# Eight weight transfers on a paced queue, and a new written-out order, in a kernel of sparse attention and a rational MLP

## The chip, the cores and the metric

The kernel runs on one core of a Trainium2 chip. The metric is the device time of one execution in microseconds. An execution profiled by the hardware gives the span from its first to its last instruction and the rows below.

## The reference

Inputs are q, k, v of shape (8 batches, 8 heads, 576 rows, 64), weights W_in (512 x 2048) and W_out (2048 x 512), and a few coefficients, all float32.

- Attention with two masks: heads 0 to 3 see the last 32 positions (the local half, L), heads 4 to 7 the positions with the same remainder modulo 32 (the strided half, S). Scores are scaled by 1/8, softmax as usual, then the product with v.
- The heads are laid side by side: x has 4608 rows of 512.
- h = x W_in; P = a0 + a1 h + a2 h^2 + a3 h^3; Q = 1 + |b0||h| + |b1| h^2; the output is (P / Q) W_out, 4608 x 512, float32.

## The kernel before

`graph` writes the work down as numbered operations with their dependences; nothing is decided at run time. Five lists (`ORDER`) give each engine its operations in order: PE (products and transposes), ACT, DVE, POOL (transfers that cast float32 to bf16) and SP (plain and transposing transfers). `SIDE` gives each movable copy, zero fill, eviction and |h| to ACT (a) or DVE (d), `AT` gives each tile in PSUM its bank. `emit` puts a semaphore wait ahead of an operation where its engine does not yet know that a dependence is done. Every engine and every queue is in order: an operation that waits holds all that stand behind it.

Batch 0 is cast straight into SBUF in two parts of 8 and 10 blocks of 32 rows and turned by PE, so is batch 1 (`stage0`, `stage1`, L379 to L446). From batch 2 on POOL casts q and k to DRAM (`casts`, L448) and v to SBUF (`casts_v`, L460), and SP loads q and k transposed (`loads`, L481) and shifts v (L473). Batch 2's casts wait for the last reader of W_in's fourth quarter in chunk 1, later ones for the loads of the batch before.

The MLP (`mlp`, L1123) works in chunks of 256, 256, then 512 rows. W_in products (L1166) fill PSUM, an eviction (helper L314) makes h; then |h| (L1184 on ACT, L1188 on DVE), Q in two DVE steps, Ln and Exp on ACT for 1/Q, P in five DVE steps, and the last product g (L1219). W_out products (L1236) follow in four operations for each 128 rows, each over 512 of the 2048 middle columns, then eviction and store (L1256).

The weights go through `weights` (L477) on POOL: W_in in four transfers of 512 columns, W_out in two of 1024 rows. A W_in operation waits for the quarter that it reads, a W_out operation for the half. None of the six transfers waits for anything but POOL's order. In that order the quarters of W_in are 21st, 25th, 30th and 31st (second, first, fourth, third), W_out's halves 34th and 37th, directly ahead of batch 2's casts.

The other early transfers, as they write bf16, by size: a cast of batch 0's q or k 128 KB (first part) or 160 (second), of batch 1's 288; a piece of V 32 or 40 for batch 0 and 72 for later ones; a quarter of W_in 512, a half of W_out 1024.

`F` and the last loop hold fill products, which compute nothing that is read; 39 of the 47 stand ahead of the first W_in product.

Of the kernel before, what the change touches and what calls it, by code (L numbers as in the profile page):

```python
# [208 lines left out]
def graph(nc, q, k, v, w_in, w_out, pa, pb, out):  # L209
# [15 lines left out]
    P = Prog(nc)  # L225
# [18 lines left out]
    Win = sb("Win", [128, NK1, Fmid])  # L244
    Wout = sb("Wout", [128, NF, Fout])
    T_win = [Tile(f"win{i}") for i in range(4)]
    T_wout = [Tile(f"wout{i}") for i in range(2)]
# [229 lines left out]
    def weights(i, into, src, T, nm, after=(), size=(512, 172)):  # L477
        P.op("pool", lambda e: e.dma_start(into, src.rearrange("(a p) n -> p a n", p=128)), "issue", (nm, i),
             w=[T[i]], dma=size, after=after)
# [647 lines left out]
    def mlp(c, t0, n, groups_):  # L1127
# [96 lines left out]
        for m in range(n // 128):  # L1224
            po = Banks(1)
            n4 = 0
            for g0, nf, h in groups:
                for j0 in range(0, nf, 4):
# [11 lines left out]
                    P.op("pe", mm, f"mm{j1 - j0}", ("w2", c, m, n4), r=[h, T_wout[(g0 + j0) // 8]], **kw)  # L1240
# [42 lines left out]
    for i in range(4):  # L1283
        weights(i, Win[:, :, hw * i:hw * i + hw], w_in[:, hw * i:hw * i + hw], T_win, "win", size=(512, 86))
    for i in range(2):
        weights(i, Wout[:, 8 * i:8 * i + 8, :], w_out[1024 * i:1024 * i + 1024, :], T_wout, "wout")
# [43 lines left out]
    for i in range(IDLE):  # L1330
# [6 lines left out]
IDLE = 47  # L1337
# [5 lines left out]
    "aadddddaaddaaddddaddaaaaadaaadddaadddaddaaadaaaadaaaaddaadadaaadaaaddadaaadadadaddaaaddaaaaaaaaaadda"  # L1343
    "daadddaaddaaaaaaaaaddaaaaaaddaaaaadaaaaaaaaadaaaaaaaadaaaaaaaaaaadaaaaaaaaaaadaaaaaadaaaaaaaaaaaaaaa"
    "aaadaaaaaadaaaadaaaaaaadaaaaadaaaaaaa--------------------d--"
# [24 lines left out]
    ),  # L1370
    "act": (
# [40 lines left out]
    ),  # L1412
}
AT = (
    "2150770154134523464752702436401010616500452342014630276345252645311531375433033565261640600773130604"
    "2664432102030151501206206461136714400711416350644073524002240040261027345113365042604231544222464642"
    "0430270113265346703751553465135314541272155526761665"
)
# [48 lines left out]
```

## Time and profile before

| | |
|---|---|
| median of 3 runs | 351.83 us (346.87 to 352.83) |
| the profiled execution | 348.38 us |
| its span | 346.5 us |
| granted TensorE clock | 1.00 over the span |
| DMA | 44.68 MB, 129 GB/s on the mean |

Busy time of an engine is the union of its instructions' durations. PE's products are pipelined and their ends modelled, so a busy PE is not PE at its peak; the step from one product to the next in the chain of waits is the better measure of what one costs. A row of a timeline gives start and duration, then engine, line, operation, out<-in by the program's names, how many instructions are merged, and in brackets the idle time of the engine before it with what ended it. Transfers issued by POOL carry the mark of the q0 queue on the page; an issue is over in under a us, its landing is a number of its own.

### The profile page before, as it was taken

What the parts mean: (1) busy time and instruction counts of PE and PEld (TensorE: products, weight loads), DVE (VectorE), ACT (ScalarE), POOL (GpSimd) and SP (SyncE); (2) the same over time, 40 slices, a digit from 0 to 9 for tenths busy, and PEclk for the clock granted to TensorE, in tenths of its full rate; (3) what the DMA queues carried; (4) which work ended last, traced back from release to release, by engine and by line L of the source; (5) the groups of instructions that cost most, each with busy time, mean ns of one, the idle gap of its engine ahead of it and who ended that gap; (6) DMA issues with size and microseconds to landing.
All of it is one profiled execution on the core that took longest, in us unless ns stands there. A gap on an engine that the chain in (4) does not pass through costs nothing.

```text
span 346.5 us, 9553 instructions
## 1 busy us (share of the span) xinstructions
PE 328.5 (95%) x4307; PEld 166.6 (48%) x4307; DVE 327.9 (95%) x300; ACT 311.1 (90%) x304; POOL 76.9 (22%) x114
## 2 busy tenths in 40 slices
PE   7888898999989999989999999999999999989896
PEld 2546675544544455444445544454445444434342
DVE  6777999999999999999999999999999999999993
ACT  6885889989989989998997999999989999999892
POOL 8990061080091027004500910000000000000000
PEclk9999999999999999999999999999999999999999
DMA  7999999998999999999999999402500200002113
GB/s 112 179 168 187 198 187 136 198 173 141 169 182 153 196 178 158 140 229 171 168 155 208 175 151 246 113 2 72 116 2 32 91 2 30 0 2 85 65 64 122
DMA packets 95370, 44.68 MB, mean 129 GB/s; under 512 B 79456, under 2 KB 89440, under 8 KB 94944
## 3 DMA queue, kind: packets, MB, share of 16 engines
q0 software_dynamic: 31584, 18.23, 41.0%
q1 hardware_dynamic: 63200, 25.69, 37.8%
q8 instruction: 34, 0.56, 0.7%
q10 hardware_dynamic: 544, 0.13, 0.2%
q14 instruction: 8, 0.07, 0.1%
HBM read 36.87 MB, written 16.52 MB: 154 GB/s over the span
## 4 chain that ended last, share of the span: by engine, by line
PE 42%; DVE 39%; ACT 14%; issue 4%; DMA 1%; DVEq 0%; ACTq 0%
PE ps L1166 16%; PE ps L1236 16%; DVE u L1194 6%; DVE z L1211 5%; DVE h L1219 5%; ACT u L1204 4%; DVE u L1191 4%; DVE z L1215 3%; ACT h L314 3%; ACT u L1199 3%; DVE z L1208 3%; PE ps L705 2%; DVE z L1213 2%; DVE z L1217 2%; DVE z L1188 1%
## 5 line engine op out<-in xcount | busy, mean ns | idle before, releaser
L1166 PE MATMUL ps<-XT,Win 128*128 128x512 bf16 (+1 forms) x640 | 132.1, 358 | 4.7 <-ACT XT L314 1.3
L1236 PE MATMUL ps<-Wout,h 128*128 128x512 bf16 x576 | 135.2, 380 | 0.7 <-issue 0.6
L1166 PEld LDWEIGHTS ps<-XT,Win 128*128 128x128 bf16 x640 | 60.7, 98 | 65.9 <-ACT h L314 2.8
L1236 PEld LDWEIGHTS ps<-Wout,h 128*128 128x128 bf16 x576 | 53.1, 98 | 60.9 <-ACT h L314 1.3
L314 ACT ACTIVATE h<-ps 128x1024 bf16<-128x1024 f32 (+2 forms) x82 | 72.0, 925 | 10.6 <-PE ps L1166 10.4
L1199 ACT ACTIVATE u<-u 128x4096 bf16<-128x4096 bf16 (+2 forms) x22 | 66.3, 3013 | 1.0 <-DVE u L1194 0.9
L1204 ACT ACTIVATE u<-u 128x4096 bf16<-128x4096 bf16 (+2 forms) x22 | 66.2, 3012 | 0.0
L1219 DVE TENSOR_TENSOR h<-z,u 128x4096 bf16<-128x4096 bf16 (+2 forms) x21 | 41.4, 1981 | 0.4
L1194 DVE TENSOR_TENSOR u<-u,z 128x4096 bf16<-128x4096 bf16 (+2 forms) x21 | 41.6, 1979 | 0.2
L1211 DVE TENSOR_TENSOR z<-z,h 128x4096 bf16<-128x4096 bf16 (+2 forms) x21 | 41.5, 1978 | 0.1
L1215 DVE TENSOR_TENSOR z<-z,h 128x4096 bf16<-128x4096 bf16 (+2 forms) x21 | 41.4, 1977 | 0.1
L400 POOL DMA_DIRECT2D vL<-in_v_dram x32 | 25.2, 791 | 62.2 <-PE ps L1236 43.4
L1184 ACT ACTIVATE z<-h 128x4096 bf16<-128x4096 bf16 (+1 forms) x13 | 36.8, 2836 | 1.0 <-DVE h L1219 0.4
L1191 DVE TENSOR_SCALAR u<-z,coef 128x4096 bf16<-128x4096 bf16 (+2 forms) x21 | 25.0, 1191 | 0.2
L391 POOL DMA_DIRECT2D vS<-in_v_dram x36 | 25.0, 699 | 0.5 <-DVE vS L343 0.5
L1208 DVE TENSOR_SCALAR z<-h,coef 128x4096 bf16<-128x4096 bf16 (+2 forms) x21 | 24.8, 1183 | 0.3
L1213 DVE TENSOR_SCALAR z<-z,coef 128x4096 bf16<-128x4096 bf16 (+2 forms) x21 | 23.6, 1124 | 0.1
L1217 DVE TENSOR_SCALAR z<-z,coef 128x4096 bf16<-128x4096 bf16 (+2 forms) x21 | 23.5, 1130 | 0.1
L314 ACT ACTIVATE os<-ps 128x512 f32<-128x512 f32 x32 | 19.7, 620 | 2.7 <-PE ps L1236 2.2
L314 ACT ACTIVATE XT<-ps 128x576 bf16<-128x576 f32 (+7 forms) x30 | 16.9, 598 | 4.3 <-PE ps L705 2.6
L1332 PE MATMUL ps<-F 128*128 128x512 bf16 x47 | 15.8, 429 | 3.4 <-DVE F L1329 2.4
L314 ACT ACTIVATE qkT<-ps 64x512 bf16<-64x512 bf16 (+6 forms) x18 | 11.0, 634 | 6.8 <-PE ps L1236 4.1
(116 smaller groups left out, 277.3 us busy)
## 6 DMA issues: line engine op xcount, KB each, us to landing
out_dram<-os SPq DMA_DIRECT2D x32, 256.0 KB, 2.8
qk<-in_q_dram POOLq DMA_DIRECT2D x12, 288.0 KB, 7.1
qk<-in_k_dram POOLq DMA_DIRECT2D x12, 288.0 KB, 7.8
Win<-in_moe_w_in_dram POOLq DMA_DIRECT2D x4, 512.0 KB, 13.3
Wout<-in_moe_w_out_dram POOLq DMA_DIRECT2D x2, 1024.0 KB, 21.9
vS<-in_v_dram POOLq DMA_DIRECT2D x28, 72.0 KB, 6.8
vL<-in_v_dram POOLq DMA_DIRECT2D x28, 72.0 KB, 6.8
vL<-vL SPq DMA_DIRECT2D x14, 138.1 KB, 3.6
```

Source lines behind the costliest of these rows:

```text
L314: return lambda e: e.tensor_copy(o_(), i_()) if e_ == "dve" else e.activation(o_(), i_(), AF.Copy)
L1166: r = e.matmul(bank(ph, 512 * (s - s0) + n * i, n), Win[:, kk, f * 128:(f + 1) * 128], XT[:, kk, x0:x0 + n], start=(kk == 0), stop=(kk == ...
L1184: P.op(e_, lambda e, z=z, h=h, i=i, hp=hp: e.activation(z.t[:, hp * i:hp * i + hp, :], h.t[:, hp * i:hp * i + hp, :], AF.Abs), f"act_{hp * ...
L1191: dv(lambda e, z=z, u=u, G_=G_: e.tensor_scalar(u.t[:, 0:G_, :], z.t[:, 0:G_, :], b1_ap, b0_ap, op0=Alu.mult, op1=Alu.add), "ts2", "u1", r ...
L1194: dv(lambda e, z=z, u=u, G_=G_: e.tensor_tensor(u.t[:, 0:G_, :], u.t[:, 0:G_, :], z.t[:, 0:G_, :], op=Alu.mult), "tt", "u2", r=[z], m=[u])
L1199: lns.append(P.op("act", lambda e, u=u, i=i, hp=hp: e.activation(u.t[:, hp * i:hp * i + hp, :], u.t[:, hp * i:hp * i + hp, :], AF.Ln, bias ...
L1204: exs.append(P.op("act", lambda e, u=u, i=i, hp=hp: e.activation(u.t[:, hp * i:hp * i + hp, :], u.t[:, hp * i:hp * i + hp, :], AF.Exp, sca ...
L1208: dv(lambda e, z=z, h=h, G_=G_: e.tensor_scalar(z.t[:, 0:G_, :], h.t[:, 0:G_, :], a_ap[3], a_ap[2], op0=Alu.mult, op1=Alu.add), "ts2", "p1 ...
L1211: dv(lambda e, z=z, h=h, G_=G_: e.tensor_tensor(z.t[:, 0:G_, :], z.t[:, 0:G_, :], h.t[:, 0:G_, :], op=Alu.mult), "tt", "p2", r=[h], m=[z])
L1215: dv(lambda e, z=z, h=h, G_=G_: e.tensor_tensor(z.t[:, 0:G_, :], z.t[:, 0:G_, :], h.t[:, 0:G_, :], op=Alu.mult), "tt", "p4", r=[h], m=[z])
L1219: dv(lambda e, z=z, h=h, u=u, G_=G_: e.tensor_tensor(h.t[:, 0:G_, :], z.t[:, 0:G_, :], u.t[:, 0:G_, :], op=Alu.mult), "tt", "g", r=[z, u], ...
L1236: r = e.matmul(bank(po, 0, Fout), hf[:, j, m * 128:(m + 1) * 128], Wout[:, kk, :], start=(kk == 0), stop=(kk == NF - 1))
```

## The change

W_out goes in four transfers of 512 rows, so the weights are eight transfers of 512 KB; a W_out operation waits for the quarter that it reads. Taken in the order W_in 0 to 3, W_out 0 to 3, each transfer waits on POOL until the one two before it has landed (`paced`). All operations behind the weights have numbers higher by two, fill products start at 1224, and there are five more of these: 41 of 52 stand ahead of the first W_in product, eleven behind it (eight before).

All five lists, `SIDE` and `AT` are new. On POOL, W_in's second quarter (39) is now 10th, its first (38) 24th, fourth (41) 26th, third (40) 29th, W_out's second (43) 32nd, first (42) 36th, fourth (45) 39th; eight casts of batch 2 follow, then W_out's third quarter (44). The casts of batch 0's first part (12 to 15) stand first. On PE, the third operation of W_out for chunk 0's first 128 rows (150 before, 152 after) now stands five W_in operations of chunk 2 behind the first two.

`SIDE` differs at 65 places. Up to the first |h|: of the start's zero fills DVE has four of 64x576, three of 64x1170, one of 128x1024 and two of 128x512 ahead of its first reduction (two, two, one and three before), with one cast of v (two before) and two evictions of batch 0's strided half (one before). On ACT, the first exponential (77 before, 79 after) stands ahead of the evictions of the local q and k of batch 0, which DVE shares. Of the first four evictions of h two are on each engine (one on DVE, three on ACT before). From the first |h| to the last g: four |h| of 4096 elements, one eviction of h of 1024, two of 320 to XT, one of 576 to qkT and two to ptL (512, 640) go from DVE to ACT; two |h| of 4096, two normalisations of 1152 (18 instructions each on ACT), one eviction of 512 to the output and two to XT (576, 640) go from ACT to DVE; others are swapped one for one. DVE's sequence of MLP steps stays nearly as it was. At the end three of the last four evictions are on DVE (one before).

```diff
-    T_wout = [Tile(f"wout{i}") for i in range(2)]
+    T_wout = [Tile(f"wout{i}") for i in range(4)]
...
     def weights(i, into, src, T, nm, after=(), size=(512, 172)):
-        P.op("pool", lambda e: e.dma_start(into, src.rearrange("(a p) n -> p a n", p=128)), "issue", (nm, i),
+        return P.op("pool", lambda e: e.dma_start(into, src.rearrange("(a p) n -> p a n", p=128)), "issue", (nm, i),
              w=[T[i]], dma=size, after=after)
...
-                    P.op("pe", mm, f"mm{j1 - j0}", ("w2", c, m, n4), r=[h, T_wout[(g0 + j0) // 8]], **kw)
+                    P.op("pe", mm, f"mm{j1 - j0}", ("w2", c, m, n4), r=[h, T_wout[(g0 + j0) // 4]], **kw)
...
-    for i in range(4):
-        weights(i, Win[:, :, hw * i:hw * i + hw], w_in[:, hw * i:hw * i + hw], T_win, "win", size=(512, 86))
-    for i in range(2):
-        weights(i, Wout[:, 8 * i:8 * i + 8, :], w_out[1024 * i:1024 * i + 1024, :], T_wout, "wout")
+    wts = [(Win[:, :, hw * i:hw * i + hw], w_in[:, hw * i:hw * i + hw], T_win, "win") for i in range(4)]
+    wts += [(Wout[:, 4 * i:4 * i + 4, :], w_out[512 * i:512 * i + 512, :], T_wout, "wout") for i in range(4)]
+    paced = []
+    for i, (into, src, T, nm) in enumerate(wts):
+        paced.append(weights(i % 4, into, src, T, nm, after=paced[i - 2:i - 1], size=(512, 86)))
...
-IDLE = 47
+IDLE = 52
...
     "pe": (
...
-        "376-377 350-351 444-447 278-279 1239 449 280 150 281 151 284 553-555 285-286 459 453 557 455 287 464 "
...
+        "339 338 150 1233 347 345 151 375-376 352 372-373 152 381-382 353 153 436-437 349 438 378 350 379 440 "
...
     "act": (
-        "35 31 216 20 9 221 8 68 70 33 36 77 66 65 63 215 90 167 82 165 89 249 96 83 217 84 172-173 19 198 "
...
+        "31 35 11 62 10 17 220 217 72 79 37 33 65 169 46 170 19 98 86 90 174 84 255 200 181 218 102 204 252 "
...
     "dve": (
-        "21-22 24 222 219 7 10 1221 25 220 23 16 60 218 18 32 61 11 37 71 75 44 78 6 79-80 17 45 168 94 223 "
...
+        "24 21 1223 25 22 7-8 221 63 20 224-225 222 23 18 16 219 223 9 32 216 70 73 77 67 80 68 81-82 172 36 "
...
     "pool": (
-        "14-15 47 12-13 46 48 163 28 51 57 55 52 29 49 53 50 161 54 56 39 27 224 26 38 231 227 160 162 41 40 "
-        "225 229 42 228 230 43 290 298 301 226 300 291 293 299 297 292 418-419 296 426 428 417 427 425 "
...
+        "14-15 12-13 49 48 50 165 51 39 56 59 52 164 55 27 58 26 28-29 54 57 53 38 163 41 233 162 40 229 227 "
+        "43 226 232 228 42 230-231 45 293-294 292 299 303 300-302 44 295 430 427 429 428 296 419-420 297 421 "
...
```

## Rows read from the trace of the kernel before

**Rows 1.** The page, its part 1 (busy us, share of the span, instructions of each engine) and the first line of its part 4 (the chain that ended last, by engine).

```profile
PE 328.5 (95%) x4307; PEld 166.6 (48%) x4307; DVE 327.9 (95%) x300; ACT 311.1 (90%) x304; POOL 76.9 (22%) x114
...
PE 42%; DVE 39%; ACT 14%; issue 4%; DMA 1%; DVEq 0%; ACTq 0%
```

**Rows 2.** The table by stage: length, then busy us (and instructions) of PE, PEld, DVE, ACT and POOL, granted clock, DMA share, GB/s.

```profile
0.00:35.00 35.00, 28.66 (x510) 17.08 (x512) 25.54 (x61) 24.92 (x44) 24.82 (x41) 1.00 1.30 162
35.00:200.00 165.00, 158.93 (x2649) 85.06 (x2643) 161.97 (x134) 151.83 (x138) 51.55 (x73) 1.00 1.15 174
200.00:305.00 105.00, 105.00 (x999) 49.33 (x997) 104.64 (x71) 101.18 (x90) 0.48 (x1) 1.00 0.31 70
305.00:325.00 20.00, 18.84 (x87) 8.15 (x87) 19.77 (x14) 19.44 (x17) 0.00 (x0) 1.00 0.13 48
325.00:346.50 21.50, 17.03 (x77) 6.93 (x74) 16.01 (x23) 13.70 (x19) 0.00 (x0) 1.00 0.24 92
```

**Rows 3.** The timeline of POOL, whose instructions issue the transfers: start us, us, engine, line, operation, tiles. In order: the first, fourth and third quarter of W_in, the second half of W_out, the first cast of batch 2 and the last of its first burst.

```profile
16.71 0.81 POOL L478 DMA_DIRECT2D Win<-in_moe_w_in_dram  x1
...
20.56 0.80 POOL L478 DMA_DIRECT2D Win<-in_moe_w_in_dram  x1
...
21.34 0.79 POOL L478 DMA_DIRECT2D Win<-in_moe_w_in_dram  x1
...
25.84 0.89 POOL L478 DMA_DIRECT2D Wout<-in_moe_w_out_dram  x1
...
46.69 0.53 POOL L450 DMA_DIRECT2D qk<-in_q_dram  x1 [19.96 <-PE ps L1166]
...
52.40 0.51 POOL L450 DMA_DIRECT2D qk<-in_q_dram  x1
```

**Rows 4.** The DMA issues by tile, asked for the stretch of one issue each (the same issues as in rows 3, the first cast of batch 2 left out): queue, operation, count, KB each, us from issue to landing.

```profile
Win<-in_moe_w_in_dram POOLq DMA_DIRECT2D x1, 512.0 KB, 12.5
...
Win<-in_moe_w_in_dram POOLq DMA_DIRECT2D x1, 512.0 KB, 14.1
...
Win<-in_moe_w_in_dram POOLq DMA_DIRECT2D x1, 512.0 KB, 15.8
...
Wout<-in_moe_w_out_dram POOLq DMA_DIRECT2D x1, 1024.0 KB, 23.7
...
qk<-in_q_dram POOLq DMA_DIRECT2D x1, 288.0 KB, 9.1
```

**Rows 5.** The timelines of PE and SP: the first products with W_in, SP's shift of batch 1's V, its user on PE, and the first products of chunk 2.

```profile
30.03 2.14 PE L1166 MATMUL ps<-XT,Win 128*128 128x256 bf16 x18 [0.40 <-ACT XT L314]
...
45.02 1.40 SPq L473 DMA_DIRECT2D vL<-vL  x2
...
56.32 0.71 PE L1081 MATMUL ps<-vL,ptL 128*32 128x130 bf16 x36 [0.35 <-DVE ptL L314]
...
61.35 5.34 PE L1166 MATMUL ps<-XT,Win 128*128 128x512 bf16 x24
```

**Rows 6.** The timelines of DVE and ACT: the first reduction, the first |h|, and the first exponential.

```profile
11.28 0.42 DVE L651 TENSOR_REDUCE ng<-ps 128x32 bf16<-128x256 f32 x1 [0.85 <-PE ps L791]
...
35.23 0.69 DVE L1188 TENSOR_SCALAR z<-h 128x2048 uint16<-128x2048 uint16 x1 [1.86 <-ACT h L314]
...
12.53 0.39 ACT L670 ACTIVATE pS<-ps 128x256 bf16<-128x256 f32 x1 [1.28 <-PE ps L658]
```

**Rows 7.** The groups of instructions by line, engine, operation and shape: count | busy us, mean ns of one | idle before. The three zero fills, |h| on either engine, the normalisation, and the evictions of 1024, 320, 576, 512 and 640 columns.

```profile
L1184 ACT ACTIVATE z<-h 128x4096 bf16<-128x4096 bf16 x9 | 32.7, 3628 | 0.2
...
L1188 DVE TENSOR_SCALAR z<-h 128x4096 uint16<-128x4096 uint16 x7 | 8.5, 1212 | 0.4 <-ACT h L314 0.4
...
L1098 DVE TENSOR_TENSOR xl<-ps,rc 128x1152 bf16<-128x1152 f32 x5 | 6.8, 1356 | 0.1
...
L343 DVE MEMSET vL<- 64x1170 f32 x2 | 2.1, 1033 | 0.5 <-issue 0.5
...
L343 DVE MEMSET qkT<- 64x576 f32 x3 | 1.6, 538 | 0.4 <-DVE Z L333 0.2 <-issue 0.2
...
L314 DVE CAST h<-ps 128x1024 bf16<-128x1024 f32 x1 | 1.2, 1218 | 0.0
...
L343 DVE MEMSET pS<- 128x512 f32 x2 | 1.0, 485 | 0.2 <-issue 0.2
...
L314 DVE CAST XT<-ps 128x320 bf16<-128x320 f32 x2 | 0.9, 487 | 0.0
...
L314 DVE COPY qkT<-ps 128x576 bf16<-128x576 bf16 x1 | 0.8, 751 | 0.0
...
L314 DVE COPY ptL<-ps 128x640 bf16<-128x640 bf16 x1 | 0.5, 480 | 0.0
...
L314 DVE COPY ptL<-ps 128x512 bf16<-128x512 bf16 x1 | 0.4, 424 | 0.0
```

**Rows 8.** The chain of waits in order of time (four products with W_in; the products behind the last h), and DVE's timeline at the end.

```profile
127.31 0.86 PE ps L1166 x4
...
340.56 2.78 PE ps L1236 x12
...
339.81 0.69 DVE L1219 TENSOR_TENSOR h<-z,u 128x1024 bf16<-128x1024 bf16 x1
342.50 0.69 DVE L314 COPY qkT<-ps 128x512 f32<-128x512 f32 x1 [1.99 <-PE ps L1236]
```

More of the change, by code (lines that the diff above doesn't have):

```diff
@@ L1342 @@
 SIDE = (
-    "aadddddaaddaaddddaddaaaaadaaadddaadddaddaaadaaaadaaaaddaadadaaadaaaddadaaadadadaddaaaddaaaaaaaaaadda"
-    "daadddaaddaaaaaaaaaddaaaaaaddaaaaadaaaaaaaaadaaaaaaaadaaaaaaaaaaadaaaaaaaaaaadaaaaaadaaaaaaaaaaaaaaa"
-    "aaadaaaaaadaaaadaaaaaaadaaaaadaaaaaaa--------------------d--"
+    "ddaadadadddadaadadadadddadadaddadddaddaddaadaaaadaadaadaddddadddaaaaaddaadadaaaaaadadadaaaaaadaaddaa"
+    "addaaaaaddaaaaaaaaaadaaaaadddaaaaadaaaaaaaaaaadaaaaaaaaaaaaaaaaaadaaaaaadaaaaaaaaaaadaaaaaaaaaaaaada"
+    "aaadaaaaaadaaaaaaaaaaadddaaaaaaaaaaaa-------------------dd-d"
 )
@@ L1414 @@
 AT = (
-    "2150770154134523464752702436401010616500452342014630276345252645311531375433033565261640600773130604"
-    "2664432102030151501206206461136714400711416350644073524002240040261027345113365042604231544222464642"
-    "0430270113265346703751553465135314541272155526761665"
+    "7145465736455160517007020634226000263417015745446610133020640616120462610514452207041426665267636224"
+    "7602446603276230025225406064506732140010626601207104322314062226403067445134213550462653244112411406"
+    "135647160021013322401160603711057220304112337662233754031"
 )
```

100 rows, old and new, of the table ORDER are left out of this document.

## The prediction

> **What bounds the kernel now.** I read the page first. TensorE, VectorE and ScalarE are all nearly full, and the chain that ended last is split between PE and DVE, with 1% on DMA [rows 1]. A mean over stages says little, so the table by stage comes next [rows 2]. Three stages are to be seen in it. Up to 35 us DVE works 25.54 us and idles 9.5: the start waits on chains of small steps. From 35 to 325 us DVE idles 3.0 + 0.4 + 0.2 = 3.6 us in all, and PE idles 6.1 + 0.0 + 1.2 = 7.2; from 200 to 305 both are full (105.00 and 104.64 of 105). Behind 325 there is a tail: DVE's last product ends at 339.81 + 0.69 = 340.50, and six us of products with W_out, eviction and store follow [rows 8].
>
> The change moves weights, so the third view is their transfers: issue on POOL's queue [rows 3], and time to landing [rows 4]. W_in's first quarter is issued at 16.71 and lands 12.5 later, at 29.2. The fourth and third land at 34.7 and 37.1, W_out's second half at 49.5. The latency grows with each issue, and the two quarters issued 0.78 apart land 2.5 apart: transfers of this queue stand in line, about 2.5 us for 512 KB. So a landing goes by the bytes ahead of it, not by its issue. Who uses them [rows 5]: the first product with W_in starts at 30.03, 0.8 behind its quarter, and the row puts its wait down to the eviction of XT. W_in's landing is thus close to binding at one place; W_out's is not (chunk 2 is at 61.35 before the third quarter of W_out matters).
>
> **The change, part by part.**
>
> *Transfers.* The second quarter of W_in goes from 21st to 10th on POOL; the bytes ahead of the first quarter's end change from 3272 to 3200 KB (the sizes named with the kernel, summed in each order), so it lands some 0.4 earlier, 28.8. All casts of batch 0's first part go first, the same bytes sooner. The pacing holds POOL: the third quarter waits for the first (28.8), W_out's first for W_in's third, and so on. Behind each of these waits stand issues of batch 1's V, and behind the last the casts of batch 2. But when POOL is released at 28.8, 1160 KB issued earlier are still in line (5.7 us at 2.5 us per 512 KB), so the line does not run dry, and landings stay where the bytes put them. Batch 1's V: 6400 KB up to its last piece against 6328, +0.4 us; SP's shift of it goes from 45.02 to 45.4 and takes five, and its user on PE stands at 56.32 [rows 5]. Cost nothing, cover 6 us. Batch 2's casts are released by POOL at about 41, where W_out's second quarter lands by the same count of bytes, and by their gate on PE at about 46.7 as before [rows 3].
>
> W_out's third quarter is now behind eight casts of batch 2. In the kernel before, the last of batch 2's casts issued in that burst lands at 52.40 + 9.1 = 61.5 with nine ahead of it [rows 3, 4]; with eight casts and its own 2.5 us the quarter lands between 60 and 64. PE needs it in the new order five operations of W_in (20 products) behind the start of chunk 2, at 61.35 + 1.1 (below) + 20 x 0.215 = 66.7 [rows 5, 8]. Cost nothing, cover 2.7 to 6.7 us; if that goes, PE stands, as its queue is in order.
>
> The Trainium skill (DMA: Bandwidth & Descriptors, "Anatomy of one DMA") gives a transfer about 2.0 us of fixed time beside its bytes. By that two transfers more would be an estimated 4 us more of line. The rows say otherwise: issued behind others, 512 KB take the 2.5 us between two landings.
>
> *Order at the start, DVE.* Before the first reduction (11.28) DVE now has two zero fills of 64x576 and one of 64x1170 more, one of 128x512 less, a cast less and an eviction more: 2 x 0.538 + 1.033 - 0.485 = +1.6 us [rows 7]; with the gaps of 0.1 to 0.25 that stand before such fills (0.5 before two, 0.4 before three), +1.9. That reduction starts at about 13.1. ScalarE's exponential, at 12.53 before, becomes about 14.4, and now stands ahead of the copies of lq on ACT's queue, so ACT idles some 5 us there instead of 1.3 [rows 6]. Behind it the zeros are done, and the moved copies nearly cancel; the four evictions of the first h are two on each engine instead of one and three. Bounds for the first |h| (35.23): 0, if the 9.5 us of idle time take it all in, to +1.9, if none. I take +1.1: the exponential and the two score products behind it are each late by the full amount, and the evener split of h returns about 0.7 (one eviction).
>
> *DVE from there to its last product.* To ACT go: four |h| of 4096 (4 x 1.212), an eviction of 1024 (1.218), two of 320 (2 x 0.487), one of 576 (0.751), two of ptL (0.424 + 0.480): 8.7 us. From ACT come: two |h| (2.424), two normalisations (2 x 1.356), an eviction of 512 (0.69), two to XT (0.48 each by ptL's row of that width): 6.8 us [rows 7, 8]. Equal swaps are left out. Net -1.9 us.
>
> *PE.* No product goes or comes but five fills: two before the first W_in, three behind. The latter cost 3 x 0.215 = 0.65 (a quarter of the chain's 0.86 for four [rows 8]) where PE is full. Bank numbers are all new; the bound for that is in the rivals.
>
> *Tail.* After the last product 12 products with W_out remain in both orders. Two more of the last four evictions are on DVE, 0.69 each (342.50, [rows 8]), spread over the products that remain. Nothing.
>
> **The sum.** If DVE sets the end: +1.1 - 1.9 = -0.8. If PE does: +1.1 + 0.65 = +1.75. Both are full from 200 to 305 [rows 2], so I take the middle, **+0.5 us**. The profiled execution took 348.38 (span 346.5 and 1.9 around it); it becomes 348.9. The median of the runs shown is 351.83, 3.45 above that execution, the lowest 1.5 below it; I add half the distance, 1.7, and predict **350.5**.
>
> **The rivals** (times on the same scale, 1.7 added).
>
> *A. The new order closes waits.* PE idles 7.2 us between 35 and 325. A better fit of order and banks could return most of that, but DVE has only 3.6 to give there, and -1.9 of work less: up to -5, 345.1. For it: DVE's shorter list. Against: the start is later, not sooner. Chance 0.14.
>
> *B. PE's waits double.* With new bank numbers a product waits until the former tile in its bank is evicted, and ACT, 92% busy from 35 to 200, is where such evictions queue. If PE's 7.2 us of idle time doubled, nothing later could take it in, since both engines are full: 357.3, slower by 2%. It decides from 7 us more of PE idle time between 35 and 325. For it: every bank and the ACT order are new, and ACT has four more |h| of 3.6 us [rows 7], less two, in front of evictions. Against: DVE's list behind 35 us keeps nearly the same sequence. Chance 0.16.
>
> *C. W_out's third quarter binds.* Issued at about 51.5, it would land at 67.3 to 68 were its latency not 9.1 and 2.5 us but 15.8, as for W_in's third quarter behind a longer line [rows 4]; PE would then stand up to 1.3 us: 351.8. For it: it is behind casts that read and write DRAM. Against: the line ahead of it is no longer than in the kernel before. Chance 0.08. The fixed time in the Trainium skill's section named above would push the same way.
>
> *D. The pacing does nothing* that can be seen in the time, since no weight ends a wait that counts. That is within the forecast; the time is then that of the new order alone.
>
> **How the numbers follow.** Forecast 0.62, its own range 347.5 to 354, from the bounds of the start (-1.1, +0.8), of DVE against PE (-1.3, +1.25), and half the spread of the runs. A and B are reached by the range: 345 to 357.3. A measurement of this kernel tells about 2%, 7 us, from no change. Faster by that: half of A and little else, 0.09. Slower: most of B and a remainder, 0.14. Within: 0.77.
>
> **What would show it.** Right: the first reduction near 13.1, the first product with W_in near 31, the first |h| near 36.3; POOL idle between issues of weights before 45 us, and no wait of PE on W_out; DVE busy about 329 us (+1.2 in all), with the last product near 341 and six us behind it. Wrong: POOL's line running dry, so that batch 1's V lands behind 50; a gap on PE ahead of the first W_out products at 60 to 70; PE idle above 14 us between 35 and 325; or the first |h| at 38 or later.

## The result, and the profile after

The changed kernel takes 352.29 us (median of 18, 350.26 to 354.61), the kernel before 350.30 on the same chip (18, 346.39 to 353.11). The ratio is 1.0104 with a 95% interval of 1.0073 to 1.0135: slower by 1%, inside the 2% within which the prediction saw no change, and yet a real loss. Ratios in this document and the counts of its last table leave out executions over 1.5% above the fastest of the same kernel (three of the 18 before, none of the 18 changed); the two medians just given hold all, and stand at 1.0057. The predicted 350.5 rests on a net change of +0.5 us.

The page of the changed kernel (span 349.2 us, the execution 351.02): part 1, the granted clock in 40 slices, and the chain by engine.

```profile
PE 326.9 (94%) x4267; PEld 167.9 (48%) x4312; DVE 330.2 (95%) x305; ACT 308.5 (88%) x265; POOL 74.3 (21%) x116
...
PEclk9789999999999999999999999999999999999999
...
DVE 42%; PE 39%; ACT 14%; issue 4%; DVEq 0%
```

The chain is shared as before [rows 1]. What is new is in the second line: the clock falls in the second and third slice. The table by stage, and the first stage cut finer (columns as in [rows 2]; the granted clock is the third number from the end):

```profile
0.00:35.00 35.00, 30.09 (x474) 16.77 (x474) 25.30 (x63) 20.97 (x35) 22.88 (x40) 0.90 1.26 169
35.00:200.00 165.00, 155.63 (x2530) 85.19 (x2548) 161.51 (x134) 150.26 (x125) 49.83 (x75) 1.00 1.09 171
200.00:305.00 105.00, 102.64 (x1103) 49.18 (x1118) 103.73 (x71) 102.61 (x74) 1.56 (x3) 1.00 0.34 68
305.00:325.00 20.00, 19.04 (x87) 8.42 (x88) 19.70 (x14) 19.97 (x15) 0.00 (x0) 1.00 0.18 66
...
12.00:20.00 8.00, 7.80 (x150) 4.33 (x150) 4.50 (x10) 4.35 (x7) 6.73 (x12) 0.57 1.46 183
```

Where it begins is on PE's timeline, with the fill products ahead of the gap and the scores behind it; then DVE's last evictions, first reduction and first |h|, and ACT's first exponential:

```profile
8.63 1.25 PE L1333 MATMUL ps<-F 128*128 128x512 bf16 x5
12.03 0.28 PE L639 MATMUL ps<-MS,IDN 128*128 128x256 bf16 x1 [2.14 <-DVE qkT L314]
...
17.54 0.63 PE L1333 MATMUL ps<-F 128*128 128x512 bf16 x1
...
32.62 1.05 PE L1166 MATMUL ps<-XT,Win 128*128 128x256 bf16 x8
```
```profile
11.15 0.54 DVE L343 MEMSET qkT<- 64x576 f32 x1 [0.17 <-issue]
11.62 0.81 DVE L314 COPY qkT<-ps 128x512 bf16<-128x512 bf16 x2
13.28 0.42 DVE L651 TENSOR_REDUCE ng<-ps 128x32 bf16<-128x256 f32 x1 [0.85 <-PE ps L791]
...
37.76 0.69 DVE L1188 TENSOR_SCALAR z<-h 128x2048 uint16<-128x2048 uint16 x1
```
```profile
14.20 0.38 ACT L670 ACTIVATE pS<-ps 128x256 bf16<-128x256 f32 x1 [4.87 <-PE ps L658]
```

PE waits 2.14 us for evictions that DVE does behind its zero fills. At 17.54 one fill product takes 0.63 us; at the full clock it takes 0.38 or 0.39. The granted clock is 0.50 there. The first |h| comes 2.53 us later than in [rows 6].

The stretch from the first |h| to the end of the last product, first of the kernel before and then of the changed one:

```profile
35.23:340.50 305.27, 296.81 (x3783) 148.18 (x3781) 301.69 (x238) 284.27 (x257) 52.03 (x73) 1.00 0.75 124
```
```profile
37.76:343.09 305.33, 291.53 (x3748) 147.80 (x3789) 301.06 (x235) 284.39 (x226) 49.40 (x74) 1.00 0.71 122
```

It is as long as before: DVE is busy 0.6 us less and waits 0.7 more (4.3 of it idle, 3.6 before). Behind it the tail is 6.10 us for 6.04. So **the span's +2.65 us is 2.53 + 0.06 + 0.06**: in these two executions all of it is there by the first |h|.

### The profile page after: what moved, and what is told of

It is laid out like the page before. It is cut to its first block, busy times and chain, and to the rows that moved or that the text cites. A ratio compares the mean times of both kernels' runs of the same rounds, so it can differ in the third digit from the quotient of the medians.

```text
span 349.2 us, 9495 instructions
## 1 busy us (share of the span) xinstructions
PE 326.9 (94%) x4267; PEld 167.9 (48%) x4312; DVE 330.2 (95%) x305; ACT 308.5 (88%) x265; POOL 74.3 (21%) x116
## 4 chain that ended last, share of the span: by engine, by line
DVE 42%; PE 39%; ACT 14%; issue 4%; DVEq 0%
PE ps L1236 15%; PE ps L1166 14%; DVE z L1211 5%; DVE u L1194 5%; DVE z L1215 5%; DVE h L1219 5%; ACT u L1199 3%; DVE z L1208 3%; ACT h L314 3%; ACT z L1184 3%; DVE u L1191 3%; DVE z L1213 3%; ACT u L1204 3%; DVE z L1217 2%; PE ps L705 2%
## 5 line engine op out<-in xcount | busy, mean ns | idle before, releaser
L1236 PE MATMUL ps<-Wout,h 128*128 128x512 bf16 x550 | 130.5, 379 | 5.1 <-issue 2.4
L1166 PEld LDWEIGHTS ps<-XT,Win 128*128 128x128 bf16 x640 | 60.1, 98 | 62.8 <-ACT h L314 4.0
L314 ACT ACTIVATE h<-ps 128x1024 bf16<-128x1024 f32 (+2 forms) x82 | 72.8, 939 | 11.3 <-PE ps L1166 10.7
L1184 ACT ACTIVATE z<-h 128x4096 bf16<-128x4096 bf16 (+1 forms) x15 | 44.1, 2950 | 1.9 <-DVE h L1219 1.7
L400 POOL DMA_DIRECT2D vL<-in_v_dram x32 | 23.5, 738 | 63.5 <-PE ps L1236 58.0
L1208 DVE TENSOR_SCALAR z<-h,coef 128x4096 bf16<-128x4096 bf16 (+2 forms) x21 | 24.6, 1181 | 0.2
L391 POOL DMA_DIRECT2D vS<-in_v_dram x36 | 22.8, 637 | 0.0
L1333 PE MATMUL ps<-F 128*128 128x512 bf16 x52 | 18.8, 461 | 1.6 <-DVE F L1330 1.2
L314 ACT ACTIVATE os<-ps 128x512 f32<-128x512 f32 x31 | 18.7, 616 | 0.7 <-PE ps L1236 0.7
L314 ACT ACTIVATE XT<-ps 128x576 bf16<-128x576 f32 (+7 forms) x30 | 16.2, 573 | 2.6 <-PE ps L1116 1.3
L314 ACT ACTIVATE qkT<-ps 64x576 bf16<-64x576 bf16 (+5 forms) x15 | 9.4, 646 | 6.7 <-PE ps L1236 3.4
```

The source lines that it names most:

```text
L314: return lambda e: e.tensor_copy(o_(), i_()) if e_ == "dve" else e.activation(o_(), i_(), AF.Copy)
L1166: r = e.matmul(bank(ph, 512 * (s - s0) + n * i, n), Win[:, kk, f * 128:(f + 1) * 128], XT[:, kk, x0:x0 + n], start=(kk == 0), stop=(kk == ...
L1184: P.op(e_, lambda e, z=z, h=h, i=i, hp=hp: e.activation(z.t[:, hp * i:hp * i + hp, :], h.t[:, hp * i:hp * i + hp, :], AF.Abs), f"act_{hp * ...
L1208: dv(lambda e, z=z, h=h, G_=G_: e.tensor_scalar(z.t[:, 0:G_, :], h.t[:, 0:G_, :], a_ap[3], a_ap[2], op0=Alu.mult, op1=Alu.add), "ts2", "p1 ...
L1236: r = e.matmul(bank(po, 0, Fout), hf[:, j, m * 128:(m + 1) * 128], Wout[:, kk, :], start=(kk == 0), stop=(kk == NF - 1))
```

## The experiments

**The changed kernel again**, unedited.

> The changed kernel once more, unedited, for a second trace of it: its executions spread from 350.3 to 354.6 us with mean clocks of 0.979 to 0.995. Theory clock: the place of the low clock is again behind the gap ahead of the first mask (13 us on), its length differs with the execution, and span minus the time of the first |h| is again 311.4 us give or take 0.5. Rival (the spread comes from later): the first |h| near 37.8 again whatever the span.

352.74 us. Its start by stretch, and the two rows that answer to those above:

```profile
10.00:12.00 2.00, 0.00 (x0) 0.00 (x0) 1.77 (x4) 0.00 (x0) 2.00 (x4) 0.88 1.38 198
12.00:20.00 8.00, 7.91 (x150) 4.33 (x150) 4.55 (x10) 4.29 (x7) 7.26 (x12) 0.50 1.44 188
20.00:26.00 6.00, 6.00 (x121) 3.81 (x125) 4.36 (x10) 3.44 (x8) 1.06 (x2) 0.57 1.39 184
```
```profile
12.03 0.40 PE L639 MATMUL ps<-MS,IDN 128*128 128x256 bf16 x1 [2.87 <-DVE qkT L314]
```
```profile
39.23 0.69 DVE L1188 TENSOR_SCALAR z<-h 128x2048 uint16<-128x2048 uint16 x1
```

PE's wait ends at 12.03 again, but it is 2.87 us long, since the fill products ahead of it end 0.7 us sooner. The clock is low for 13.6 us (0.5 + 8.0 + 5.2, each stretch by twice what its clock lacks to 1) instead of 6.9, and the first |h| is 1.47 us later still. Span minus first |h| is 311.7 (311.4 in the first trace): these two executions differ at the start and hardly behind it.

**The transfers alone.** First in the changed kernel, without pacing:

```diff
-        paced.append(weights(i % 4, into, src, T, nm, after=paced[i - 2:i - 1], size=(512, 86)))
+        paced.append(weights(i % 4, into, src, T, nm, size=(512, 86)))
```

> The changed kernel without the pacing: the eight transfers wait for nothing but POOL's order, everything else as it is. Theory start: the same as the changed kernel, ratio to the kernel before 1.007 to 1.013, the first reduction still at 13.3 and the first |h| near 37.8. Rival transfers (POOL waiting 13 us for landings costs the time): ratio 0.998 to 1.004.

1.0130 (1.0065 to 1.0194): nothing comes back. Its trace is a third of the same lists. PE's gap is 2.44 us, the clock is low for 3.4 us, and the first |h| is the earliest of the three:

```profile
12.00:20.00 8.00, 7.73 (x179) 4.69 (x180) 6.22 (x12) 4.55 (x8) 8.00 (x14) 0.79 1.44 188
```
```profile
36.91 0.69 DVE L1188 TENSOR_SCALAR z<-h 128x2048 uint16<-128x2048 uint16 x1
```

Then the kernel before with the eight paced transfers and the new POOL list, its other lists kept:

> The kernel before with the change's transfers alone: eight paced transfers and the new POOL list; the lists of PE, ACT, DVE and SP, the sides and the banks stay those of the kernel before. Theory start: no difference, ratio 0.997 to 1.003, first reduction at 11.3, first |h| at 35.2, W_in's first quarter landing near 24.7 as in the changed kernel. Rival transfers: slower by the whole difference, ratio 1.007 to 1.013, with a wait of PE on a quarter of W_out or of W_in in the trace.

1.0050 (1.0005 to 1.0095), between the two forecasts. The profiled execution was the slowest of the twelve. In it PE waits for a load, and POOL's later order, made for other lists, is the likely reason (us in total, times, longest):

```profile
PE ps L639 <- DMA qkT<-qk: 3.3, 1, 3.3
```

So POOL's order from batch 2 on was put back, and the eight transfers kept at their new places:

> The kernel before with the eight paced transfers placed on POOL among batch 0's and 1's casts as in the changed kernel (W_out's third quarter behind eight casts of batch 2), while POOL's order of the casts from batch 2 on stays that of the kernel before. In the first kernel with the change's transfers alone the first |h| came at 34.5, sooner than before, but PE stood 3.3 us on a load of q and k near 90 us, which belongs to POOL's later order, made for other lists. Theory start: no such stall, first |h| 34.5 to 35.3, ratio to the kernel before 0.997 to 1.003. Rival transfers: 1.005 to 1.010, PE or SP waiting on landings all along.

1.0013 (0.9967 to 1.0059), span 345.5; W_in's first product and the first |h|:

```profile
29.95 0.72 PE L1166 MATMUL ps<-XT,Win 128*128 128x256 bf16 x5 [0.40 <-ACT XT L314]
```
```profile
34.38 0.69 DVE L1188 TENSOR_SCALAR z<-h 128x2048 uint16<-128x2048 uint16 x1 [1.10 <-ACT h L314]
```

That wait is gone from this trace, but the intervals of the two runs overlap, so what POOL's later order costs is not settled. The transfers cost nothing that shows (at most 0.6%, 2 us, by the interval), and in this trace the first |h| is even 0.85 us earlier: [rows 5] begin W_in's products at 30.03 and lose 0.60 of idle time among them, which is gone here.

**The clock.** Nine fill products more in PE's gap (`new` numbers 1276 on):

```diff
-  ... 1256 1230 74-76 66 78 ...
+  ... 1256 1230 1276-1284 74-76 66 78 ...
```

> The changed kernel with nine more fill products (1.9 us at the full clock) on PE directly ahead of the first mask of the strided half, where PE stood idle for 2.14 us and behind which its granted clock read 0.50 from 13 to 19.2 us. Theory clock (the late start costs most of what it costs through the clock): the granted clock from 12 to 20 us reads 1.00 instead of 0.57, the first |h| comes near 36.3 instead of 37.76, the time is some 1.4 us below the changed kernel, a ratio to the kernel before of 1.005 to 1.007, and the executions lie closer together than 350.3 to 354.6. Rival (the clock only slows work that has slack): clock back, the first |h| stays near 37.8 and the ratio at 1.010.

1.0055 (1.0015 to 1.0095). In the profiled execution 1.32 us of gap were left, the clock was 0.50 from 16 to 20 us, and the first |h| came at 37.90. So with twelve:

> As the changed kernel with nine more fill products ahead of the first mask, but twelve: in the trace with nine, PE still idled 1.32 us there and the clock fell to 0.5 from 13.9 to 20 us, while five of its twelve executions had a mean clock of 1.00 and spans of 347.5 to 348.2. Theory clock: the gap closes to under 0.7 us, granted clock 1.00 over the first 40 us, first |h| at 36.4 to 36.9 (the late first reduction at 13.3 stays), spans of 347.3 to 348.3 in most executions, ratio to the kernel before 1.003 to 1.007. Rival: the first |h| stays at 37.5 or later with the clock at 1.00.

1.0063 (1.0018 to 1.0108). Only four of the twelve executions kept a mean clock of 0.998 or more (five with nine), where most were expected to. But this trace has a start at the full clock. A row of PE, one of DVE, and stretches:

```profile
12.03 0.28 PE L639 MATMUL ps<-MS,IDN 128*128 128x256 bf16 x1 [0.37 <-DVE qkT L314]
```
```profile
36.30 0.95 DVE L1188 TENSOR_SCALAR z<-h 128x2048 uint16<-128x2048 uint16 x1
```
```profile
12.00:20.00 8.00, 6.87 (x180) 4.20 (x180) 5.94 (x13) 5.14 (x9) 7.25 (x12) 1.00 1.46 184
...
50.00:60.00 10.00, 7.74 (x147) 5.56 (x148) 9.68 (x14) 9.35 (x12) 2.78 (x5) 0.94 1.49 136
60.00:70.00 10.00, 10.00 (x49) 4.78 (x48) 8.25 (x7) 5.88 (x5) 0.00 (x0) 0.89 0.95 198
```

With the first reduction as late as ever (13.28) and the clock whole, the first |h| is at 36.30 instead of 37.76 or 39.23. Further on the clock fell all the same, behind PE's 2.3 idle us at 50 to 60, and DVE idled 1.75 of the ten us from 60; it fell again between 95 and 110 (0.89). The span is 351.4.

Five traces now share the changed lists and the late reduction, so the first |h| can be set beside the time at the low clock: 36.30 (none), 36.91 (3.4 us), 37.76 and 37.90 (6.9 each), 39.23 (13.6), which is 0.18 to 0.24 us for each us. The four with a low clock at the start then take 305.3 to 305.9 us to the last product, as the kernel before does (305.3): what is late at the first |h| is late at the end.

The reverse is a gap made in the kernel before by leaving out eight of its fill products (`1238 1265`, `1240`, `1259 1247 1227 1267 1246`):

> The kernel before without the eight fill products that stand between its first turns and the subtraction of the first maximum; nothing else is touched and the output does not depend on them. PE then idles about 1.9 us in two stretches between 9.3 and 12.2 us. Theory clock (PE's idle time at the start, not the changed order as such, lowers its clock, and that costs time): granted clock near 0.5 for 3 to 8 us behind 12 us, first |h| at 36.0 to 36.6 instead of 35.2, nearly all executions with a mean clock of 0.995 or less, ratio to the kernel before 1.003 to 1.008. Rival (fills compute nothing and the chain of scores does not wait for them): clock 1.00, ratio 0.998 to 1.002.

1.0040 (0.9980 to 1.0100), eleven of twelve executions with a mean clock of 0.995 or less. In the trace, PE, a stretch, and the first |h|:

```profile
10.49 0.72 PE L791 MATMUL ps<-qkT 128*8 128x16 bf16 x64 [1.32 <-DVE qkT L314]
```
```profile
12.00:22.00 10.00, 10.00 (x127) 6.21 (x127) 5.78 (x16) 7.29 (x15) 8.06 (x13) 0.51 1.65 162
```
```profile
36.77 0.69 DVE L1188 TENSOR_SCALAR z<-h 128x2048 uint16<-128x2048 uint16 x1 [1.10 <-ACT h L314]
```

The ratio alone is unclear; the trace shows the start. Behind a gap of 1.32 us the clock is at half for ten, and the first |h| comes 1.54 us later, though nothing that is read was touched. The span is 351.0, so 2.9 us more are lost behind the first |h|; there PE has gaps of 1.35 and 1.29 us at 103 and 119, and the clock stays at 1.00.

**Evictions ahead of zero fills** (70, 73: evictions; 77: the first reduction; 219, 223, 9, 216: zero fills; 32: a cast):

```diff
-  ... 16 219 223 9 32 216 70 73 77 67 80 68 81-82 172 ...
+  ... 16 70 73 223 9 77 219 67 80 68 81-82 32 216 172 ...
```

> The changed kernel with one edit to DVE's list at the start: the two evictions of batch 0's strided half and the reduction behind them go ahead of three zero fills and a cast. Theory start (late evictions on DVE hold the chain of scores, and PE's gap lowers the clock): the first mask on PE at about 9.9 instead of 12.03, the first reduction at 11.1 instead of 13.28, the exponential at 12.3 instead of 14.20, clock 1.00 over the first 20 us, the first |h| between 35.2 and 36.0, ratio to the kernel before 0.997 to 1.003. Rival transfers or rival order behind 38 us (the loss is in the weights, or in the new lists later on): ratio stays at 1.007 to 1.013 whatever the first reduction does.

First reduction 11.34, exponential 12.14, first mask 10.03, all as said; but first |h| only at 36.50 and the ratio 1.0066 (1.0024 to 1.0107), since PE now had a gap of 1.23 us behind 13.9 and the clock was 0.63 from 16 to 20 us. With ten fill products in its gaps:

> The kernel with evictions ahead of zero fills at the start, and ten fill products more in the three gaps of PE that its profile shows (0.50 us ahead of the first subtraction of the maximum, 1.23 ahead of the first turn of the strided half, 0.66 ahead of the second mask), behind which its clock read about 0.5 from 16.9 to 20 us. Theory clock: granted clock 1.00 up to 24 us, the first |h| at 35.4 to 36.0 instead of 36.5, most executions with a mean clock of 1.00, ratio to the kernel before 1.000 to 1.004. Rival: the clock falls all the same, ratio 1.005 to 1.010.

Clock 1.00 throughout, nine of twelve executions at 0.998 or more, ratio 1.0052 (1.0017 to 1.0087). The first |h| is at 36.22, against 36.30 with the late reduction: **at the full clock the zero fills cost almost nothing.** What holds the first |h| is further on, in PE's order; a turn of batch 1 waits, for its bank, ahead of the strided scores (the row of PE; the first |h| and a later one on DVE behind it):

```profile
21.17 0.42 PE L572 MATMUL ps<-IDN,h 72*128 72x72 bf16 x8 [0.95 <-DVE u L314]
```
```profile
36.22 0.69 DVE L1188 TENSOR_SCALAR z<-h 128x2048 uint16<-128x2048 uint16 x1
...
250.94 1.23 DVE L1188 TENSOR_SCALAR z<-h 128x4096 uint16<-128x4096 uint16 x1 [0.94 <-ACT h L314]
```

That wait undone (on PE the scores 177, 178 ahead of the turn 253; on ACT 19 ahead of 46, 174 ahead of 86):

> The kernel with evictions ahead of zero fills and ten more fill products, with its chain of scores freed: on PE the second part's strided scores go ahead of a turn of batch 1's k, which waited 0.95 us there; on ACT a zero fill goes ahead of the shift of V that waits 2.5 us, and an eviction of the second part's k ahead of two copies of u. Theory order: these scores start at 20.4 to 21.2 instead of 22.17, the second strided reduction at 21.8 to 22.6 instead of 23.51, the first |h| at 34.8 to 35.5 instead of 36.2. Rival (the W_in products' places and banks hold the first |h|): first |h| still at 36.0 or later.

The scores start at 20.53 and the first |h| comes at 35.23, as the theory said, but the span is 349.5 (347.3 without this edit). From first |h| to last product it takes 308.16 us instead of 305.0, with waits of 1.20 and 2.06 us on DVE ahead of 168 and 182.5, and a granted clock of 0.97 from 150 to 200. The W_in products freed instead:

> The same base, its W_in products freed instead: the four of the first |h| stand nearly together on PE, the last of them takes bank 7 and no longer waits for copies of u out of bank 6, and DVE's eviction of it and the first |h| go ahead of three of these copies. Theory order: first W_in product unchanged at 31.1, from it to the first |h| 4.4 to 4.8 us instead of 5.14, so the first |h| at 35.5 to 35.9 instead of 36.2. Rival (the chain of scores alone counts): 36.2.

A miss: first |h| at 36.61, 0.4 later than without the edit, and behind it PE waits 1.37 us for copies of u that the edit put back. Both together, and both with more fill products:

> Both edits together. Theory order: first |h| at 34.1 to 35.0, as with the old order and the same transfers (34.4); span 345.3 to 346.5 in executions with a mean clock of 1.00; ratio to the kernel before 0.996 to 1.003, so that the changed kernel's loss is gone with its lists behind the start untouched. Rival order behind the start: the first |h| is early, but ratio stays at 1.004 to 1.008, the gain lost again behind 38 us.

> The same, with seven fill products in three gaps of PE between 42 and 59 us (0.6 us ahead of the second batch's strided maximum, 0.5 ahead of its local one, 0.9 ahead of the first W_out products). Theory clock: no execution's clock falls at 50 to 67 us as it did in one trace (0.89 there); mean clock 1.00 in nearly all, ratio 0.5 to 2 thousandths lower than without these fills, 0.994 to 1.001. Rival (fills only add 1.5 us of PE's work): 1 to 4 thousandths higher.

First |h| at 35.09 and 34.61, ratios 1.0065 (1.0026 to 1.0104) and 1.0094 (1.0057 to 1.0132). An early first |h| brought nothing in these two: part of the work that stood ahead of it now stands behind (DVE is busy 302.0 us there in the last, 300.8 without these edits), and the waits behind it grow. One of them stands ahead of the same products in both, for copies of u that the edit put back (for each a row of PE, then a stretch):

```profile
36.70 0.83 PE L751 MATMUL ps<-u,vS 128*64 128x40 bf16 x32 [1.35 <-DVE u L314]
35.00:41.00 6.00, 4.65 (x84) 3.57 (x82) 5.66 (x10) 4.09 (x9) 1.89 (x3) 0.72 1.51 173
```
```profile
36.15 0.69 PE L751 MATMUL ps<-u,vS 128*64 128x40 bf16 x32 [1.29 <-DVE u L314]
35.00:41.00 6.00, 4.85 (x156) 4.14 (x157) 5.80 (x11) 5.42 (x10) 2.23 (x3) 1.00 1.52 168
```

In the first the clock falls behind it (0.72 over these six us), in the second it does not, nor behind the 1.37 us above. So the length of a gap alone does not say whether the clock falls.

**The start swapped** between the two kernels, cut at the first |h|:

> All of the change but the start: PE, ACT, DVE and SP have the operations up to the first |h| in the order, on the engines and in the banks of the kernel before, and from there the changed kernel's; transfers and POOL as changed. Theory start (everything is lost ahead of the first |h|): first |h| at 34.5 to 35.9, granted clock 1.00 up to 40 us, ratio to the kernel before 0.998 to 1.003. Rival order behind the start (the new lists from 38 us on cost about 2 us, which the one profile of the kernel before hides): first |h| as early, but ratio 1.005 to 1.009.

> The mirror: the changed kernel up to the first |h|, then the lists, sides and banks of the kernel before; transfers as changed, POOL's later casts as before. Theory start: first reduction at 13.3, PE idle 2 us ahead of the first mask, granted clock near 0.5 for some us behind it, first |h| at 37 to 38, ratio to the kernel before 1.007 to 1.013. Rival order behind the start: ratio 1.001 to 1.005, the first |h| late all the same.

1.0105 (1.0054 to 1.0156) and 1.0172 (1.0099 to 1.0245), the second from three of its six executions. The first ratio speaks against the theory that everything is lost at the start, the second against its rival, and neither start came as early as said. Most likely the seam has costs of its own, which no run separates. With the old start the first |h| came at 36.13, and the clock fell to 0.71 from 60 to 65 us, behind 1.3 idle us of PE in the five before; all six executions had a mean of 0.995 or less. With the new start the first |h| was at 39.31.

**The kernel before with the new transfers and fuller gaps:**

> The kernel before with the eight paced transfers at the start (as in the second such kernel: first |h| 34.4, span 345.5) and seven fill products more in five gaps of PE of 0.29 to 0.74 us between 14 and 26 us, on banks that are free. If the gaps are what lets the clock fall in about a third of the executions of the kernel before (mean clock 0.995, spans of 347.6 to 351), nearly all executions have a mean clock of 1.00 and spans of 344 to 346.5, ratio 0.990 to 0.998. Rival (those executions are late for another reason, behind the start): ratio 0.998 to 1.003, with the same third at 0.995.

The trace is as hoped (first |h| 34.38, clock 1.00, span 346.2), but of six executions three had a mean clock of 0.99 to 0.995, where nearly none was expected to, and the times go from 346.74 to 355.70, too far apart for a ratio. Where the kernel before loses its clock, in 15 of 73 executions, isn't known.

**Executions sorted by clock.** Each execution gives its span and its mean granted clock:

| kernel | executions, median span | with a mean clock of 0.998 or more |
|---|---|---|
| before (four series) | 73, 346.4 | 58, 345.6 |
| before, new transfers (second) | 9, 346.2 | 8, 345.9 |
| changed | 18, 350.5 | none |
| changed, nine or twelve fill products | 24, 349.2 | 9, 347.8 |
| the same with evictions first and ten | 12, 347.6 | 9, 347.4 |
| both start edits on that, without and with fills | 24, 349.6 | 8, 348.2 |

The changed kernel's own executions go with the clock too: 348.7 (three, 0.995), 350.3 (five, 0.989 to 0.990), 351.2 (ten, below). With its gap filled and the clock whole its lists take 347.8: **2.7 us of its median go with the clock**, between the 1.46 and 2.93 us that the two traces lost at the start. The other **2.2 us (347.8 against 345.6) remain at the full clock** and, as the transfers cost nothing that shows, belong to the new lists. The four series are from four chips; on one chip at a time these are 2.1 us with nine fill products and 1.6 with twelve. The kernel before loses 0.8 us of its own median in the same way (346.4 against 345.6).

Sorting is no experiment, though. The 15 executions of the kernel before with a lower clock (all at 0.994 or 0.995, so 3.5 to 4.2 us at half) have a median of 349.0, which is 3.4 us above the others; the 0.18 to 0.24 us for each us found at the start would make that 1.0 at most. So an execution can be late for another reason that also leaves PE idle. And at the full clock the spans of the kernel before still go from 344.4 to 349.6.

## Why the prediction was wrong

Two terms of the sum failed. The start's +1.1 priced at nothing what PE loses while it waits, and DVE's -1.9 was taken as time in full.

- **Transfers: cost nothing.** Right within the intervals of the two runs above. W_out's third quarter, issued at 52.67, landed 10.1 later at 62.8 (predicted 60 to 64); its user on PE stands at 67.26 (66.7), with no wait on W_out in the trace. W_in's first quarter landed sooner than counted (issued at 15.53, landed 9.1 later, at 24.6; 28.8 predicted and 29.2 before), though the bytes issued ahead of it are nearly the same: a landing does not go by these bytes alone. Whether that is why W_in's products lost their break is not shown. The Trainium skill's fixed 2.0 us for each transfer (DMA: Bandwidth & Descriptors, "Anatomy of one DMA") did not show: the interval of 0.9967 to 1.0059 leaves room for 2 us, not for the estimated 4.
- **Start on DVE: +1.9 us to the first reduction, +1.1 to the first |h|.** The reduction (13.28, predicted 13.1), the exponential (14.20; 14.4) and ACT's idle 4.87 (5) came as counted. The first |h| at the full clock came at 36.30, as predicted to the digit, but by luck, not for the reason given: putting the evictions ahead of the zero fills moved it by 0.08.
- **The term that was missing** is what PE does while DVE is late. The prediction gave ACT's idle time there and priced PE at nothing. PE idled 2.14 us, the granted clock went to 0.50, its lower level of 1.2 GHz, and +1.1 became +2.5 in one trace and +4.0 in the other: 1.46 us for 6.9 us at the low clock, 2.93 for 13.6. The Trainium skill (TensorE: Matmul & The Clock Gate, "What's actually happening") says that activity releases the throttle and that there are two levels only; the rows agree as to the levels, 0.50 and 1.00 with mixtures where a stretch holds both. [Rows 2] read 1.00 in every stage, and the prediction has no word on the clock.
- **DVE from the first |h| to its last product: -1.9.** The stretch measured +0.06. The moved work went as counted: by the groups of both profiles |h| of 4096 went from 7 to 5 (8.5 to 6.0 us), normalisations from 5 to 7 (6.8 to 9.5), and the durations of all DVE instructions in the stretch add up to 316.7 us before and 314.8 after. But a duration is not a step: where the next instruction follows at once, its row begins some 0.08 us before the last one ends (11.15 + 0.54 is past 11.62 in the rows above). That is so at 181 places before and 168 after, and the overlaps went from 15.0 to 13.7 us. So DVE's busy time, the union, fell by 0.6 only, and over the span it is 330.2 and not 329. And 0.7 of waiting came in. One wait is the new order's own: the |h| shown at 250.94 stands 0.94 us for ACT's evictions, and it does so for 0.84 to 0.94 us in all twelve traces with the changed lists from the first |h| on; the kernel before idles 0.4 us in all from 250 to 300. That this term would be gained in full needed every wait and every overlap to stay as it was, and no row was given for that.
- **PE-set, +1.75, and the middle taken between both.** Which engine sets the end the chain does not settle (DVE 42%, PE 39%). Both bounds hold the start's term, which is paid whatever engine rules later and was too small in both.
- **Rival B, PE's waits double.** It came near in the first trace, 12.7 us of idle time between 35 and 325 (9.4 + 2.4 + 1.0) where double is 14.4. But that trace lacks matmul records: it has 4267, the second trace of the same kernel 4312, which is the 4307 of the kernel before and the five fill products. The second has 5.7 + 0.7 + 0.9 = 7.3, as before. Neither A nor C happened; D did. The start of part 1 of the second trace's page, and its stages:

```profile
PE 334.0 (95%) x4312; PEld 169.1 (48%) x4312; DVE 330.6 (94%) x305; ACT 308.6 (88%) x265; POOL 75.7 (22%) x116
...
35.00:200.00 165.00, 159.26 (x2567) 85.93 (x2565) 161.28 (x136) 149.42 (x126) 49.21 (x72) 1.00 1.11 169
200.00:305.00 105.00, 104.34 (x1119) 49.18 (x1117) 103.74 (x72) 102.42 (x73) 3.17 (x6) 1.00 0.37 70
305.00:325.00 20.00, 19.15 (x90) 8.46 (x88) 19.67 (x13) 19.80 (x17) 0.00 (x0) 1.00 0.18 66
```

- **Tail: nothing.** Right, 6.1 for 6.0 us, with three evictions on DVE.

That 352.29 lies in the stated range says little, as half the spread of the runs was in that range.

What stays open: how the 2.2 us at the full clock divide between the order of the start and the lists behind it. By the traces 1.07 of them are there at the first |h| (36.30 for 35.23). But freeing the start alone did not return them, and swapping the starts seems to have added costs of the seam.

## What to carry to other kernels

When a step on one engine is made later, price what the waiting TensorE loses besides the wait: here a gap of 2.1 to 2.9 us ahead of a chain of small products was followed by 3 to 14 us at half the clock, and that more than doubled a delay of 1.1 us. Fill products in such a gap are part of the schedule, and a new order has to place them anew. Work moved off an engine is worth its steps, not its durations. Look at the mean clock of every execution before comparing medians, but don't take every late execution with a low clock for one that is late by the clock, nor an early milestone for an early end.

## Unexpected on the hardware

- The length of the low clock does not go with the length of the gap ahead of it: at the same place in the same lists gaps of 2.14, 2.44 and 2.87 us were followed by 6.9, 3.4 and 13.6 us of it. Mean clocks were 0.979 to 0.995 in the 18 executions of the changed kernel, none at 1.00.
- Gaps of 1.23, 1.32 and 1.35 us were followed by the low clock too, while others of 1.29 to 1.93 us, further on in the traces, were not. The largest of the kernel before at its start, 0.74, was not in its trace.
- In the first trace 1% of the matmul records were missing, enough to fake 5 us of idle time on PE.
- One execution of the kernel with the changed start and the old lists took 1817 us; why is not known.
